# Decode attention with a gated feed-forward: load placement, half-head multiplies, normalisation in pairs and the order of the last loads

## The chip, the cores and the metric

The kernel runs on one core of a Trainium2 chip. The core has a matrix engine (TensorE, "PE" in the profile, its weight loads "PEld"), a vector engine (VectorE, "DVE"), a scalar engine (ScalarE, "ACT"), GpSimd ("POOL") and SyncE ("SP"), which here issues nearly all transfers. Sixteen DMA engines move data between the main memory (HBM) and the on-chip memory (SBUF: 128 partitions); matmul results go to PSUM. The engines run at the same time and wait for each other through semaphores. The metric is the time of one execution on the device in microseconds, as the median of several runs.

## The reference

```python
xn = layernorm(x)                                  # x: 4 x 1 x 640
q = (xn @ wq).reshape(B, 1, 32, 192)               # 32 heads of 192
k, v = k_cache[:, :, 8192 - 2048:, :], v_cache[:, :, 8192 - 2048:, :]
scores = einsum("bhqd,bhkd->bhqk", q, k) * 192 ** -0.5
o = einsum("bhqk,bhkd->bhqd", softmax(scores), v)
A = o.reshape(B, 1, 32 * 192) @ wo
Bf = (silu(xn @ w1) * (xn @ w3)) @ w2              # 640 -> 1536 -> 640
out = x + A + Bf
```

All inputs are bf16. Each of the 4 batch rows has its own K and V for each of 32 heads, and the last 2048 positions count. Per head that is 3 MiB of K and 3 MiB of V for all batch rows, and each is used once.

## The kernel before

The 2048 positions of 4 batch rows lie on 128 partitions: 32 partitions per batch row, 64 positions on each. One head's K is a buffer `kt` of 128 x 64 x 192 (24576 bytes a partition), its V a buffer `vt`; there are two of each, used in turn. The program writes out every engine's order by hand; nothing is scheduled for it.

SP issues the loads (lines 173 to 202). First the projection weights: `wq` into `vt` and `prs` (the product buffer), `w1`, `w3` and `w2` into `wts`; then K0, K1, V0; then for each head h the pair K(h+2), V(h+1), with the first five groups of `wo` put in behind heads 4, 6 and 8; then V31 in two halves and the last three groups of `wo` into `kt0`. `load_k` (L161) waits until three reduces of the head that used the buffer are done, `load_v` (L169) until that head's P x V product is done. The queue is in order: a load that waits holds up all behind it.

The start computes the layer norm on VectorE (L234 to L242, in buffers `xf`, `xc`, `sq`), the transposed input, q for all heads broadcast over the partitions (`qbc`), and the feed-forward, whose result is added up in the PSUM bank `acc` together with x.

Then each head runs through these steps:

- VectorE multiplies a quarter of K by q (`mult`, L266, 128 x 3072), in the two halves of `prs` in turn.
- TensorE adds up the 192 columns to 32 by six matmuls with the identity (`adder`, L435 to L441) into one of two PSUM banks `ps`; VectorE adds up the last 32 (`reduce_quarter`, L273) to 16 scores a partition.
- The maximum: VectorE over the partition (`chain_lmax`, L278), TensorE transposes it (`tr`, L445), VectorE takes the maximum of each batch row and scales it (`chain_gmax`, L282 and L285), TensorE broadcasts it (`bc`, L449), ScalarE copies it (L369).
- ScalarE takes the exponential with its sum (L371), VectorE spreads it into `z` (`chain_z`, L292), TensorE adds up the sums (`tot`, L453) and multiplies `z` by V (`pv`, L458, 32 matmuls).
- ScalarE copies the product (L374); TensorE gathers it by selector matmuls (`osum`, L472, in fp32) into `po`, where the two heads of a pair have columns of their own; VectorE normalises each head (`norm_rec`, L299, `norm_og`, L305) into 32 rows of `og`, and after four heads transposes `og` into `oT` (L309).
- TensorE multiplies `oT` by a group of `wo` into `acc` (`proj`, L399, 12 matmuls a group). Groups 0 to 4 lie among the last two heads (L506 to L525), 5 to 7 behind the last one (L541 to L551).

The steps of one head are put between those of the next: VectorE takes the maximum of head h-1 between the quarters of head h, and the loop of TensorE (L494 to L504) does the same for 28 heads, with the first and the last ones written out. At the very end VectorE copies `acc` to `res` (L352), and SP and ScalarE store half of the columns each (L201, L376). `take` (L138) waits for a semaphore and counts it down again, in an instruction of its own. Semaphores from `s_first` to `s_last` are cleared at the end by GpSimd.

Of the kernel before, what the change touches and what calls it, by code (L numbers as in the profile page):

```python
# [16 lines left out]
def kernel(  # L17
# [58 lines left out]

    kt = [sb(f"kt{i}", [P, NJ, Dh], BF16) for i in range(2)]
    vt = [sb(f"vt{i}", [P, NJ, Dh], BF16) for i in range(2)]
    prs = sb("prs", [P, 2, JQ, Dh], BF16)
# [3 lines left out]
    xf = sb("xf", [B, D], FP32)  # L83
    xc = sb("xc", [B, D], FP32)
    sq = sb("sq", [B, D], FP32)
# [9 lines left out]
    tot_w = sb("tot_w", [P, PB, B], FP32)  # L95
    sel_w = sb("sel_w", [P, 2, PB, B], FP32)
# [12 lines left out]
    rt = sb("rt", [P, 2], FP32)  # L109
# [11 lines left out]
    def sem(name):  # L121
# [4 lines left out]
     s_gp, s_dv, s_ac, s_pp, s_ps, s_red, s_tr, s_gmax, s_bc, s_negm, s_exp, s_pv, s_sum, s_rec, s_og, s_oT,  # L126
     s_tot) = [sem(n) for n in (
        "s_x", "s_wq0", "s_wq1", "s_wq2", "s_w1", "s_w3", "s_w2", "s_k0", "s_k1", "s_v31", "s_wom", "s_wo5",
        "s_wo6", "s_wo7a", "s_wo7b", "s_gp", "s_dv", "s_ac", "s_pp", "s_ps", "s_red", "s_tr", "s_gmax", "s_bc",
        "s_negm", "s_exp", "s_pv", "s_sum", "s_rec", "s_og", "s_oT", "s_tot")]  # L130
    last = sem("s_last")
    s_pr, s_lmax, s_gneg, s_z, s_v0, s_v1, s_osb, s_acc, s_fin, s_out0, s_out1 = [sem(n) for n in (
        "s_pr", "s_lmax", "s_gneg", "s_z", "s_v0", "s_v1", "s_osb", "s_acc", "s_fin", "s_out0", "s_out1")]
# [6 lines left out]
    def flat(t):  # L140
        return t[:].rearrange("p a b -> p (a b)")

    wq_rows = [flat(vt[k // 2])[:, (k % 2) * H * Dh:(k % 2 + 1) * H * Dh] for k in range(4)]
    wq_rows.append(prs[:].rearrange("p a j d -> p (a j d)"))
# [13 lines left out]
    def load_k(h):  # L158
        if h >= 2:
            sp.wait_ge(s_red, 4 * (h - 2) + 3)  # L160
        sp.dma_start(out=flat(kt[h % 2]), in_=k_win[:, h].rearrange("b (p j) d -> p b (j d)", p=PB)).then_inc(s_k[h % 2], 16)  # L161
# [20 lines left out]
    for h in range(H - 2):  # L182
        load_k(h + 2)
        if h + 1 < H - 1:
            load_v(h + 1)
        if h in (4, 6, 8):
            g = h - 4
            n = 2 if g < 4 else 1
            sp.wait_ge(s_pp, 16)
            sp.dma_start(out=wts[g // 2][:, 0:n * RPP * D].rearrange("p (g i) -> p g i", g=n),  # L190
                         in_=A_wo[g * QW:(g + n) * QW, :].rearrange("(g p i) n -> p g (i n)", g=n, i=RPP)).then_inc(s_wom, 16)
    load_v(H - 1, 0, NJ // 2)
    load_v(H - 1, NJ // 2, NJ, s_v31)
    sp.wait_ge(s_red, 4 * (H - 2) + 3)
# [5 lines left out]
    take(sp, s_fin, 1)  # L200
    sp.dma_start(out=out_v[:, 0:N0], in_=res[0:B, :]).then_inc(s_out0, 16)  # L201
    take(sp, s_out0, 16)
# [21 lines left out]
    dv(ve.memset, one[:], 1.0)  # L224
    dv(ve.memset, acc[:, 0:N0], 0.0)
# [4 lines left out]
    dv(ve.tensor_copy, out=tot_w[:], in_=mask_f[:].unsqueeze(1).to_broadcast([P, PB, B]))  # L230
    for par in range(2):
        dv(ve.tensor_copy, out=sel_w[:, par], in_=rows[:, par * B:(par + 1) * B].unsqueeze(1).to_broadcast([P, PB, B]))
    ve.wait_ge(s_x, 16)
    dv(ve.tensor_copy, out=xf[:], in_=x_sb[:])  # L234
    dv(ve.tensor_reduce, out=ssum[:], in_=xf[:], axis=AX.X, op=ALU.add)
    dv(ve.tensor_scalar_mul, out=negmean[:], in0=ssum[:], scalar1=-1.0 / D)
    n_xc = dv(ve.tensor_scalar_add, out=xc[:], in0=xf[:], scalar1=negmean[:, 0:1])
# [4 lines left out]
    n_xn = dv(ve.tensor_scalar_mul, out=xn[:], in0=xc[:], scalar1=rstd[:, 0:1])  # L242
# [19 lines left out]
    def mult(u):  # L262
        h, g = u // GQ, u % GQ
        if g == 0:
            ve.wait_ge(s_k[h % 2], 16 * (h // 2 + 1))
        ve.tensor_tensor(out=prs[:, u % 2], in0=kt[h % 2][:, g * JQ:(g + 1) * JQ, :],  # L266
                         in1=qbc[:, h * Dh:(h + 1) * Dh].unsqueeze(1).to_broadcast([P, JQ, Dh]),
                         op=ALU.mult).then_inc(s_pr, 1)

    def reduce_quarter(u):  # L270
        h, g = u // GQ, u % GQ
        ve.wait_ge(s_ps, u + 1)
        ve.tensor_reduce(out=sc[h % 3][:, g * JQ:(g + 1) * JQ], in_=ps[u % 2][:].rearrange("p (j d) -> p j d", d=DD),  # L273
                         axis=AX.X, op=ALU.add).then_inc(s_red, 1)

    def chain_lmax(h):
        ve.wait_ge(s_red, GQ * (h + 1))
        ve.tensor_reduce(out=lmax[h % 2][:], in_=sc[h % 3][:], axis=AX.X, op=ALU.max).then_inc(s_lmax, 1)  # L278

    def chain_gmax(h):  # L280
        ve.wait_ge(s_tr, h + 1)
        ve.tensor_reduce(out=gmax[h % 2][:], in_=mt[0:1, 0:P].rearrange("o (p b) -> o b p", b=B), axis=AX.X,  # L282
                         op=ALU.max).then_inc(s_gmax, 1)
        ve.wait_ge(s_gmax, h + 1)
        ve.tensor_scalar_mul(out=gneg[h % 2][:], in0=gmax[h % 2][:].unsqueeze(1).to_broadcast([1, PB, B]),  # L285
                             scalar1=-SCALE).then_inc(s_gneg, 1)

    def chain_z(h):
        if h >= 2:
            ve.wait_ge(s_pv, h - 1)  # L290
# [4 lines left out]
    def po_of(h):  # L295
        return po if h < H - 2 else tb

    def norm_rec(c0, c1):
        ve.reciprocal(out=rt[:, c0:c1], in_=po[:, 2 * Dh + c0:2 * Dh + c1]).then_inc(s_rec, c1 - c0)  # L299

    def norm_og(h):
        sl = slice((h % HG) * CT, (h % HG + 1) * CT)
        ve.wait_ge(s_sum, h + 1)
        ve.wait_ge(s_rec, h + 1 if h >= H - 2 else h // 2 * 2 + 2)
        ve.tensor_scalar_mul(out=og[sl].rearrange("p i r -> p (i r)"), in0=po_of(h)[sl, (h % 2) * Dh:(h % 2 + 1) * Dh],  # L305
                             scalar1=rt[sl, h % 2:h % 2 + 1]).then_inc(s_og, 1)
        if h % HG == HG - 1:
            ve.wait_ge(s_og, h + 1)
            ve.transpose(out=oT[:, h // HG].rearrange("p i r -> p (i r)"), in_=flat(og)).then_inc(s_oT, 1)  # L309

    def norm(i):
        ve.wait_ge(s_sum, 2 * i + 2)
        norm_rec(0, 2)
        norm_og(2 * i)
        norm_og(2 * i + 1)

    for h in range(H):
        u, hp = h * GQ, h - 1
        if h < H - 1:
            mult(u)  # L320
        if h:
            reduce_quarter(u - 1)
            chain_lmax(hp)
        if h == H - 1:
            chain_gmax(hp)
            chain_z(hp)
            mult(u)
        mult(u + 1)
        reduce_quarter(u)
        if 0 < h < H - 1:  # L330
            chain_gmax(hp)
        mult(u + 2)
        reduce_quarter(u + 1)
        if h % 2 and 1 < h < H - 1:
            norm(h // 2 - 1)
        if 0 < h < H - 1:
            chain_z(hp)
        mult(u + 3)
        reduce_quarter(u + 2)
    norm(NP - 2)  # L340
    reduce_quarter(H * GQ - 1)
    chain_lmax(H - 1)
    chain_gmax(H - 1)
    ve.wait_ge(s_tot, 1)
    norm_rec(0, 1)
    norm_og(H - 2)
    chain_z(H - 1)
    ve.wait_ge(s_tot, 2)
    norm_rec(1, 2)
    norm_og(H - 1)  # L350
    take(ve, s_acc, 1)
# [6 lines left out]
    ae.activation(out=sq[:], in_=xc[:], func=ACTF.Square, accum_out=ssq[:]).then_inc(s_ac, 1)  # L358
# [8 lines left out]
    for h in range(H):  # L367
        ae.wait_ge(s_bc, h + 1)
# [6 lines left out]
    take(ae, s_fin, 1)  # L375
    ae.dma_start(out=out_v[:, N0:D], in_=res[CT:CT + B, :]).then_inc(s_out1, 16)  # L376
    take(ae, s_out1, 16)


    take(gp, s_fin, 1)  # L380
# [54 lines left out]
    def adder(g):  # L435
        take(pe, s_pr)
        pe.ldweights(idb[:])  # L437
        pr = prs[:, g % 2]
# [8 lines left out]
    def bc(par):  # L447
        take(pe, s_gneg)
        pe.matmul(mt[:, P:P + 1], lhsT=gneg[par][:].rearrange("o p b -> o (p b)"), rhs=one[:], start=True,  # L449
                  stop=True).then_inc(s_bc, 1)  # L450

    def tot(par):
        return pe.matmul(po[:, 2 * Dh + par:2 * Dh + par + 1], lhsT=flat(tot_w), rhs=rsum[par][:], start=True, stop=True)  # L453

    def pv(par, j0=0, j1=NJ):
        for jj in range(j0 // 2, j1 // 2):
# [6 lines left out]
    def tot_pv(par):  # L463
        take(pe, s_z)
        tot(par)
        take(pe, s_v[par], 16)
        pv(par)

    def osum(par, bank):
        take(pe, s_osb)  # L470
        for k in range(2):
            m = pe.matmul(bank[:, par * Dh:(par + 1) * Dh], lhsT=sel_w[:, k].rearrange("p a b -> p (a b)"),  # L472
                          rhs=o_sb[par][:, k * Dh:(k + 1) * Dh].rearrange("p (r i) -> p i r", i=RPP), start=(k == 0), stop=(k == 1))
# [8 lines left out]
    for g in range(5):  # L482
        adder(g)
# [4 lines left out]
    tot_pv(0)  # L488
# [5 lines left out]
    with pe.While(lambda: pe.snap(cnt) < NP - 1):  # L494
        for par in range(2):
            adder(0)
            tr(1 - par)
            osum(par, po)
# [3 lines left out]
            tot_pv(1 - par)  # L502
            adder(3)
        pe.reg_add(cnt, cnt, 1)  # L504

    pe.wait_ge(s_wom, 48)  # L506
    pe.wait_ge(s_oT, 5)
    adder(0)
    tr(1)
    osum(0, po)  # L510
    adder(1)
    bc(1)
    proj(0)
    adder(2)
    tot_pv(1)
    adder(3)
    proj(1)
    tr(0)
    bc(0)
    osum(1, po)  # L520
    proj(2)
    proj(3)
    adder(0)
    adder(1)
    proj(4)  # L525
    adder(2)
    take(pe, s_z)
    take(pe, s_v0, 16)
    pv(0)
    adder(3)  # L530
    osum(0, tb)
    tr(1)
    tot(0).then_inc(s_tot, 1)
    bc(1)
    take(pe, s_z)
    tot(1).then_inc(s_tot, 1)
    take(pe, s_v1, 16)
    pv(1, 0, NJ // 2)
    pe.wait_ge(s_v31, 16)
    pv(1, NJ // 2, NJ)  # L540
    pe.wait_ge(s_oT, 7)  # L541
    pe.wait_ge(s_wo5, 16)
    osum(1, tb)
# [38 lines left out]
```

## Time and profile before

| | us |
|---|---|
| median of 3 runs (lowest, highest) | 532.81 (532.72, 533.38) |
| the profiled execution | 532.96 |
| its span, first to last instruction | 530.8 |
| busy: PE, PEld | 358.6, 99.0 |
| busy: VectorE, ScalarE | 361.7, 44.4 |
| bytes read from HBM | 222.96 MB, 420 GB/s over the span |

The profile is one execution. Its page has busy times, the span in 40 slices, the DMA queues and the costliest groups of instructions; other views list instructions in order of time, waits, and busy times of a chosen window. A group's line names its source line, engine and operation, what it writes and reads, shape and count, then busy us and mean ns of one, then the engine's idle time before it and what ended most of that. The granted clock is the share of full speed that TensorE is given; over the span it was 0.858.

### The profile page before, as it was taken

The numbers are of one execution on the slowest core, as the hardware profiler recorded it, in microseconds if no ns is written. First come the engines' busy times: TensorE is split into PE (matmuls) and PEld (weight loads), VectorE is DVE, ScalarE is ACT, GpSimd is POOL, SyncE is SP. The second block draws the span as 40 slices with busy tenths as digits, with TensorE's granted clock in tenths as the row PEclk, the third lists the DMA queues.
The fourth block names the chain that finished last, engine by engine and source line by source line (L and its number), as shares of the span: only waits on it lengthen the run. The fifth ranks groups of instructions, "written<-read, shape, count | busy, mean of one in ns | idle before, by whom it ended". The sixth has DMA issues, their size and how long they took to land. (4 is left out here: it accounts for less than half of the span.)

```text
span 530.8 us, 5131 instructions
## 1 busy us (share of the span) xinstructions
PE 358.6 (68%) x2306; PEld 99.0 (19%) x1617; DVE 361.7 (68%) x468; ACT 44.4 (8%) x142; POOL 1.1 (0%) x8
## 2 busy tenths in 40 slices
PE   2664767767387473777667666677777667666996
PEld 0010112112022121222111121122221112121323
DVE  3135878768377584768777676767778677767781
ACT  2120100000000000000000000000001000000100
POOL 0000000000000000000000000000000000000000
PEclk9896997878878697888978788888879778889997
DMA  8999999999999999999999999999999999999993
GB/s 356 421 438 425 427 429 428 437 424 423 436 435 421 437 417 436 433 426 435 428 433 430 435 428 430 431 428 433 428 433 426 433 428 431 430 430 433 429 414 132
DMA packets 11522, 223.08 MB, mean 420 GB/s; under 512 B 1260, under 2 KB 1400, under 8 KB 2424
## 3 DMA queue, kind: packets, MB, share of 16 engines
q1 hardware_dynamic: 11496, 222.96, 98.3%
q8 instruction: 4, 0.07, 0.0%
q14 instruction: 6, 0.05, 0.0%
q10 hardware_dynamic: 16, 0.01, 0.0%
HBM read 222.96 MB, written 0.01 MB: 420 GB/s over the span
## 5 line engine op out<-in xcount | busy, mean ns | idle before, releaser
L387 PE MATMUL ps<-prs,idb 128*128 128x512 bf16 x768 | 222.5, 433 | 135.3 <-PEq L138 135.3
L266 DVE TENSOR_TENSOR prs<-kt,qbc 128x3072 bf16<-128x3072 bf16 x128 | 223.7, 1749 | 102.7 <-DMA kt<-in_A_k_cache_dram 102.7
L273 DVE TENSOR_REDUCE sc<-ps 128x16 f32<-128x512 f32 x128 | 87.9, 687 | 18.1 <-PE ps L387 17.0
L437 PEld LDWEIGHTS <-idb 128*128 128x128 bf16 x128 | 13.1, 102 | 197.3 <-issue 195.6
L458 PE MATMUL o_ps<-vt,z 128*8 128x384 bf16 x1024 | 47.3, 327 | 0.0
L472 PE MATMUL po<-o_sb,sel_w 128*128 128x192 f32 x120 | 46.3, 519 | 0.0
L369 ACT COPY negm<-mt 128x1 f32<-128x1 f32 x32 | 5.1, 159 | 347.4 <-PE mt L449 347.4
L472 PEld LDWEIGHTS po<-o_sb,sel_w 128*128 128x128 f32 x120 | 31.0, 286 | 11.0 <-issue 7.0
L458 PEld LDWEIGHTS o_ps<-vt,z 128*8 128x8 bf16 x1024 | 22.0, 86 | 14.2 <-issue 1.3
L374 ACT COPY o_sb<-o_ps 128x384 f32<-128x384 f32 x32 | 15.3, 479 | 101.6 <-PE o_ps L458 101.6
L449 PEld LDWEIGHTS mt<-one,gneg 1*128 1x128 f32 x64 | 9.4, 182 | 58.1 <-issue 58.1
L453 PE MATMUL po<-rsum,tot_w 128*128 128x1 f32 x64 | 10.9, 239 | 12.9 <-PEq L138 12.9
L453 PEld LDWEIGHTS po<-rsum,tot_w 128*128 128x128 f32 x64 | 9.9, 188 | 51.2 <-issue 51.1
L292 DVE TENSOR_TENSOR z<-ex,mask_b 128x256 bf16<-128x256 bf16 x32 | 13.2, 414 | 6.3 <-ACT ex L371 6.0
L220 DVE CAST qbc<-ps 128x512 bf16<-128x512 f32 x2 | 1.4, 692 | 19.1 <-PE ps L387 19.1
L305 DVE TENSOR_SCALAR og<-po,rt 32x192 bf16<-32x192 f32 x30 | 12.4, 413 | 2.1
L445 PEld LDWEIGHTS mt<-idf,lmax 128*1 128x1 f32 x32 | 3.6, 113 | 50.5 <-issue 50.5
L449 PE MATMUL mt<-one,gneg 1*128 1x1 f32 x64 | 12.0, 255 | 1.3 <-PEq L138 1.3
L445 PE MATMUL mt<-idf,lmax 128*1 128x128 f32 x32 | 12.2, 380 | 0.2 <-PEq L138 0.2
L371 ACT ACTIVATE ex<-sc,negm 128x64 bf16<-128x64 f32 x32 | 11.2, 349 | 1.0
L387 PE MATMUL ps<-vt,xnT 128*128 128x512 bf16 x15 | 6.2, 504 | 5.4 <-DMA vt<-in_A_wq_dram 3.8
L282 DVE TENSOR_REDUCE gmax<-mt 1x4 f32<-1x128 f32 x32 | 8.6, 270 | 1.0 <-PE mt L445 1.0
(70 smaller groups left out, 94.8 us busy)
## 6 DMA issues: line engine op xcount, KB each, us to landing
kt<-in_A_k_cache_dram SPq DMA_DIRECT2D x32, 3072.0 KB, 18.0
vt<-in_A_v_cache_dram SPq DMA_DIRECT2D x31, 3072.0 KB, 24.7
vt<-in_A_wq_dram SPq DMA_DIRECT2D x2, 3072.0 KB, 13.4
wt<-in_B_w_dram SPq DMA_DIRECT2D x3, 1920.0 KB, 28.1
wt<-in_A_wo_dram SPq DMA_DIRECT2D x2, 1920.0 KB, 31.2
vt<-in_A_v_cache_dram SPq DMA_DIRECT2D x2, 1536.0 KB, 16.8
kt<-in_A_wo_dram SPq DMA_DIRECT2D x2, 960.0 KB, 20.7
prs<-in_A_wq_dram SPq DMA_DIRECT2D x1, 1536.0 KB, 20.0
```

What stands on the lines that cost most here:

```text
L266: ve.tensor_tensor(out=prs[:, u % 2], in0=kt[h % 2][:, g * JQ:(g + 1) * JQ, :], in1=qbc[:, h * Dh:(h + 1) * Dh].unsqueeze(1).to_broadcast( ...
L273: ve.tensor_reduce(out=sc[h % 3][:, g * JQ:(g + 1) * JQ], in_=ps[u % 2][:].rearrange("p (j d) -> p j d", d=DD), axis=AX.X, op=ALU.add).the ...
L292: ve.tensor_tensor(out=z[h % 2][:], in0=ex[h % 2][:].unsqueeze(2).to_broadcast([P, NJ, B]), in1=mask_b[:].unsqueeze(1).to_broadcast([P, NJ ...
L305: ve.tensor_scalar_mul(out=og[sl].rearrange("p i r -> p (i r)"), in0=po_of(h)[sl, (h % 2) * Dh:(h % 2 + 1) * Dh], scalar1=rt[sl, h % 2:h % ...
L374: ae.copy(out=o_sb[h % 2][:], in_=o_ps[h % 2][:, 0:2 * Dh]).then_inc(s_osb, 1)
L387: return pe.add_instruction(mybir.InstMatmult(name=nc.get_next_instruction_name(), engine=pe.engine, ins=[pe.lower_ap(rhs), pe.lower_ap(lh ...
L437: pe.ldweights(idb[:])
L445: pe.transpose(out=mt[0:1, 0:P], in_=lmax[par][:], identity=idf[:]).then_inc(s_tr, 1)
L449: pe.matmul(mt[:, P:P + 1], lhsT=gneg[par][:].rearrange("o p b -> o (p b)"), rhs=one[:], start=True, stop=True).then_inc(s_bc, 1)
L453: return pe.matmul(po[:, 2 * Dh + par:2 * Dh + par + 1], lhsT=flat(tot_w), rhs=rsum[par][:], start=True, stop=True)
L458: m = pe.matmul(o_ps[par][c * CT:c * CT + 2 * B, 0:2 * Dh].rearrange("p (a d) -> p a d", a=2), lhsT=z[par][:, 2 * jj:2 * jj + 2, :], rhs=v ...
L472: m = pe.matmul(bank[:, par * Dh:(par + 1) * Dh], lhsT=sel_w[:, k].rearrange("p a b -> p (a b)"), rhs=o_sb[par][:, k * Dh:(k + 1) * Dh].re ...
```

## The change

- A pad in front of the buffers puts `kt0`, and with it all loaded buffers, at a multiple of 512 bytes in each partition. `xf`, `xc` and `sq` now lie in `qbc`, which is written later.
- `prs` is twice as large. A multiply covers half a head (128 x 6144), and `s_m` counts multiplies. `load_k` waits for the two multiplies of the head that used the buffer. TensorE's `adder` no longer waits for the multiply itself but for the reduce behind it in VectorE's order (`s_pr` for quarters 0 and 2).
- The scaling of the maximum goes from VectorE to ScalarE, behind a wait for `s_gmax`.
- The sums and the selector products of two heads are added up in the same PSUM columns, each head in its own 32 rows (`tot_w` and `sel_w` have zeros elsewhere), so that one reciprocal and one 64-row multiplication normalise both.
- K31 is issued behind K30, ahead of V29 and V30. TensorE's written-out end has another order: the projection of group 0 ahead of V29's product, groups 1 to 4 around the last head's maximum.
- The last waits (`s_acc`, `s_fin`) stand in the instructions that need them; the counting down comes after the store.

```diff
+    sb("pad", [P, -((nc.sbuf_base + 31) // 32 * 32) % 512 // 2], BF16)
     kt = [sb(f"kt{i}", [P, NJ, Dh], BF16) for i in range(2)]
     vt = [sb(f"vt{i}", [P, NJ, Dh], BF16) for i in range(2)]
-    prs = sb("prs", [P, 2, JQ, Dh], BF16)
+    prs = sb("prs", [P, 2, 2, JQ, Dh], BF16)
...
-    xf = sb("xf", [B, D], FP32)
-    xc = sb("xc", [B, D], FP32)
-    sq = sb("sq", [B, D], FP32)
+    xf, xc, sq = [qbc[0:B, 2 * i * D:2 * (i + 1) * D].bitcast(FP32) for i in range(3)]
...
     def load_k(h):
         if h >= 2:
-            sp.wait_ge(s_red, 4 * (h - 2) + 3)
+            sp.wait_ge(s_m, 2 * (h - 2) + 2)
...
     for h in range(H - 2):
         load_k(h + 2)
-        if h + 1 < H - 1:
+        if h < H - 4:
             load_v(h + 1)
...
+    load_v(H - 3)
+    load_v(H - 2)
     load_v(H - 1, 0, NJ // 2)
     load_v(H - 1, NJ // 2, NJ, s_v31)
-    sp.wait_ge(s_red, 4 * (H - 2) + 3)
+    sp.wait_ge(s_m, 2 * (H - 2) + 2)
...
-    take(sp, s_fin, 1)
+    sp.wait_ge(s_fin, 1)
     sp.dma_start(out=out_v[:, 0:N0], in_=res[0:B, :]).then_inc(s_out0, 16)
+    take(sp, s_fin)
...
+    dv(ve.memset, tot_w[:], 0.0)
+    dv(ve.memset, sel_w[:], 0.0)
...
     for par in range(2):
-        dv(ve.tensor_copy, out=sel_w[:, par], in_=rows[:, par * B:(par + 1) * B].unsqueeze(1).to_broadcast([P, PB, B]))
+        dv(ve.tensor_copy, out=quads(tot_w[:, par], par), in_=mask_f[:].unsqueeze(1).unsqueeze(1).to_broadcast([P, 2, PQ, B]))
+        for k in range(2):
+            dv(ve.tensor_copy, out=quads(sel_w[:, par, k], par),
+               in_=rows[:, k * B:(k + 1) * B].unsqueeze(1).unsqueeze(1).to_broadcast([P, 2, PQ, B]))
...
+    def mult(h, a):
+        if a == 0:
             ve.wait_ge(s_k[h % 2], 16 * (h // 2 + 1))
+        ve.tensor_tensor(out=prs[:, a].rearrange("p q j d -> p (q j) d"), in0=kt[h % 2][:, 2 * a * JQ:2 * (a + 1) * JQ, :],
+                         in1=qbc[:, h * Dh:(h + 1) * Dh].unsqueeze(1).to_broadcast([P, 2 * JQ, Dh]),
+                         op=ALU.mult).then_inc(s_m, 1)
...
+    def norm_rec(i):
+        ve.reciprocal(out=rt[:], in_=tb[:, 0:1]).then_inc(s_rec, 1)
+
+    def norm_og(i):
+        sl = slice(i % 2 * 2 * CT, (i % 2 + 1) * 2 * CT)
+        ve.wait_ge(s_rec, i + 1)
+        ve.tensor_scalar_mul(out=og[sl].rearrange("p i r -> p (i r)"), in0=po[sl, 0:Dh], scalar1=rt[sl, 0:1]).then_inc(s_og, 1)
...
     for h in range(H):
+        mult(h, 0)
         if h:
+            reduce_quarter(h - 1, 2)
+            reduce_quarter(h - 1, 3)
+            chain_lmax(h - 1)
+        mult(h, 1)
+        if h:
+            chain_gmax(h - 1)
+        reduce_quarter(h, 0)
+        reduce_quarter(h, 1)
+        if h % 2 and h > 1:
+            norm_rec(h // 2 - 1)
+            norm_og(h // 2 - 1)
+        if h:
+            chain_z(h - 1)
...
-    take(ve, s_acc, 1)
+    ve.wait_ge(s_acc, 1)
...
     for h in range(H):
+        ae.wait_ge(s_gmax, h + 1)
+        ae.mul(out=gneg[h % 2][:], in_=gmax[h % 2][:].unsqueeze(1).to_broadcast([1, PB, B]), mul=-SCALE).then_inc(s_gneg, 1)
         ae.wait_ge(s_bc, h + 1)
...
     def adder(g):
-        take(pe, s_pr)
+        if g % 2 == 0:
+            take(pe, s_pr)
+        add_up(g)
+
+    def add_up(g):
         pe.ldweights(idb[:])
-        pr = prs[:, g % 2]
+        pr = prs[:, g // 2, g % 2]
...
+    adder(0)
+    tr(1)
+    osum(0)
+    adder(1)
+    bc(1)
+    adder(2)
+    tot(1)
+    adder(3)
     pe.wait_ge(s_wom, 48)
     pe.wait_ge(s_oT, 5)
+    proj(0)
+    pv(1)
     adder(0)
+    tr(0)
+    osum(1)
+    adder(1)
+    bc(0)
+    adder(2)
+    tot(0)
+    adder(3)
+    pv(0)
+    proj(1)
     tr(1)
+    proj(2)
     bc(1)
+    osum(0)
     proj(3)
     proj(4)
     tot(1).then_inc(s_tot, 1)
     pv(1, 0, NJ // 2)
     pe.wait_ge(s_v31, 16)
     pv(1, NJ // 2, NJ)
+    osum(1)
     pe.wait_ge(s_oT, 7)
     pe.wait_ge(s_wo5, 16)
-    osum(1, tb)
     proj(5)
```

## The prediction

> **What bounds the kernel now.** I read the transfer rows first, because the slices show them full from end to end.
>
> ```profile
> DMA  8999999999999999999999999999999999999993
> GB/s 356 421 438 425 427 429 428 437 424 423 436 435 421 437 417 436 433 426 435 428 433 430 435 428 430 431 428 433 428 433 426 433 428 431 430 430 433 429 414 132
> ...
> q1 hardware_dynamic: 11496, 222.96, 98.3%
> ...
> q14 instruction: 6, 0.05, 0.0%
> ```
>
> Only the first and the last slice fall away; SP's queue (q1) keeps 16 engines 98.3% busy. By the landings of consecutive loads, 3 MiB take 7.304 us again and again (8 packets of 24576 bytes per engine, 912 ns each, plus one of 4 bytes, 9 ns). A head is a K and a V, 14.6 us. Next, who could starve that queue:
>
> ```profile
> SPq L161 <- DVE sc L273: 417.4, 30, 21.6
> ...
> SPq L169 <- PE o_ps L458: 11.4, 1, 11.4
> ...
> L266 DVE TENSOR_TENSOR prs<-kt,qbc 128x3072 bf16<-128x3072 bf16 x128 | 223.7, 1749 | 102.7 <-DMA kt<-in_A_k_cache_dram 102.7
> ...
> L305 DVE TENSOR_SCALAR og<-po,rt 32x192 bf16<-32x192 f32 x30 | 12.4, 413 | 2.1
> ```
>
> SP waits for VectorE to release a K buffer, yet the engines never pause, since a load still runs when the next is issued; VectorE itself waits 102.7 us for K. So VectorE, TensorE and ScalarE time inside the 30 middle heads is worth nothing. What is left is the bytes' rate, and the end, read in short windows (columns: length, busy us and counts of PE, PEld, DVE, ACT, POOL, granted clock, DMA share, GB/s) and in the timeline:
>
> ```profile
> 520.00:522.00 2.00, 1.33 (x14) 0.78 (x7) 0.00 (x0) 0.48 (x1) 0.00 (x0) 0.54 0.76 306
> 522.00:523.00 1.00, 1.00 (x5) 0.49 (x6) 0.00 (x0) 0.00 (x0) 0.00 (x0) 0.50 0.24 95
> 523.00:524.00 1.00, 1.00 (x10) 0.46 (x9) 0.81 (x2) 0.00 (x0) 0.00 (x0) 0.50 0.06 26
> 524.00:525.00 1.00, 1.00 (x10) 0.46 (x8) 0.00 (x0) 0.00 (x0) 0.00 (x0) 0.50 0.06 23
> 525.00:526.00 1.00, 1.00 (x10) 0.53 (x8) 0.00 (x0) 0.00 (x0) 0.00 (x0) 0.50 0.00 0
> ```
>
> ```profile
> 518.99 1.65 PE L458 MATMUL o_ps<-vt,z 128*8 128x384 bf16 x32
> ...
> 520.68 0.48 ACT L374 COPY o_sb<-o_ps 128x384 f32<-128x384 f32 x1 [2.65 <-PE o_ps L458]
> ...
> 521.30 1.68 PE L472 MATMUL tb<-o_sb,sel_w 128*128 128x192 f32 x4 [0.67 <-PEq L138]
> 522.91 4.59 PE L399 MATMUL acc<-kt,oT 128*4 128x320 bf16 x36
> ...
> 527.65 0.48 DVE L352 CAST res<-acc 36x320 bf16<-36x320 f32 x1 [3.79 <-DVEq L138]
> 528.25 0.35 SPq L201 DMA_DIRECT2D out_dram<-res  x1
> ```
>
> From 523 to 525 a share of 0.06 is one engine of 16: one runs late by 2.1 us. The last weights (issued at 502.92, 22.6 us to landing) are there at 525.5, but TensorE ends at 527.5: from 520.16 it has half the clock, and 36 matmuls take 4.59 us. At the full clock 12 of these took 0.98 and 24 took 1.79, so 36 would take 2.6.
>
> **The change, part by part.** The sum is made against the profiled execution, 532.96 us (span 530.8, 2.2 around it), 0.15 above the median of 532.81.
>
> *Work taken off VectorE: 0.* Two multiplies of 6144 for four of 3072 save about 0.08 a head (two in a row took 3.42, not 2 x 1.75); the scaled maximum goes to ScalarE (32 x 215 ns less); one 64-row normalisation replaces two of 32 (half of 12.4 us). All lies under VectorE's 102.7 us of waiting for K. A head needs about 2 x 3.42 + 4 x 0.69 + 0.22 + 0.27 + 0.41 + 0.4 = 10.9 us of 14.6. The price of coarser pieces is that TensorE's first sum starts 1.7 us later after a landing, inside the spare 3.7 us; beyond that it would be paid each head. ScalarE's new wait for the maximum stands behind the copy of the previous head's output and before the negated maximum and the exponential, which TensorE's order needs in that sequence anyway.
>
> *Buffers released by the multiply:* K is free about 8.4 us after its landing (3.42 + 1.6 of reduces and maximum + 3.42) rather than about 11. Nothing, since no engine pauses now.
>
> *Prelude: 0.* Two memsets and four more small copies (about 0.2-0.3 each, as L220's rows) put roughly 1.3 us before the layer norm. TensorE there waited 1.26 us for the first weights, which covers it but for 0.1; the next weights come 7 us later and swallow that.
>
> *Multiples of 512.* The program's addresses put kt0 at 16512 = 32 x 512 + 128 and every loaded buffer at the same remainder; a pad of 384 bytes makes it 0. No run here has a load at remainder 0. Bound: packets of 24576 and 12288 bytes took 912 and 460 ns, so a packet costs 2 x 460 - 912 = 8 ns beyond its bytes (27.2 GB/s per engine). Each engine moves 10240 / 16 = 640 packets: at most 5.1 us to gain. The other end is 0: the 4-byte packets cost 9 ns with nothing to place. A loss I exclude, as all buffers move together. The nearest rows are 1280-byte packets to two places, 53 ns (x, remainder 128) and 55 ns (end of the last weights, 384): 2 ns. I take 2 x 640 = **-1.3 us**.
>
> [...]
>
> *Fewer instructions: -0.9 us.* VectorE's list goes from 560 to 376. Instruction packets of 8192 bytes came at 192, 311 and 428 us, about every 130 VectorE instructions; beside each, one data packet took about 1570 ns for 912, and the fetch 325: 1.0 us on the late engine. At 10.3 instead of 15.6 instructions a head there are two, not three, before the end. Ends: 0 (ScalarE's 32 more fetched there too) and -1.0.
>
> *K31 before V29, and TensorE's new end: -1.4 us.* The two swap places: K31 lands near 496.5, V29 at 503.9 (K31's place, issued 486.98, 16.9 to landing). Queues: K31's issue needs both multiplies of head 29, 474.6 + 8.4 = 483.0, first packet 1.0 later (as at the start, issue 0.96, first packet 2.0); the quick engines finish K30 at 484.9, 0.9 to spare, the late one 2.2 more. V31 stands behind V29's product on SP, and the last weights behind V31: V29 503.9 + 1.5, first packet 506.4, V30 done at 506.8 on the quick engines. Tight, but the late engine sets the end. Then TensorE by start to start in the timeline (product 1.41, sum 1.30, selector sum 1.34, transpose 0.18, broadcast 0.30, total 0.28, projection 0.81): from 503.94, product 29, four sums, transpose, selector sum and broadcast, with the wait for z, bring the last sum to an end at 512.9; product 30 514.3; projection 1, transpose, projection 2, broadcast 516.4; selector sum 517.8; projections 3 and 4 519.4; total, product 31 521.1; ScalarE's copy 521.7; selector sum 523.3; 36 matmuls 525.8. The last weights at 525.1 and 525.5 then hold it to about 526.1, for 527.5. V31's wait is gone from this chain; the weights' landing is late next.
>
> This needs the full clock. In these windows of 3.41 us the clock falls after one with little TensorE work:
>
> ```profile
> 472.37:475.78 3.41, 0.00 (x0) 0.00 (x0) 1.14 (x1) 0.00 (x0) 0.00 (x0) 1.00 0.99 425
> ...
> 513.34:516.75 3.41, 3.08 (x17) 1.29 (x8) 2.14 (x7) 0.48 (x1) 0.00 (x0) 1.00 1.00 417
> 516.75:520.16 3.41, 1.80 (x36) 1.27 (x36) 1.21 (x5) 0.60 (x3) 0.00 (x0) 1.00 1.02 422
> 520.16:523.57 3.41, 2.74 (x18) 1.48 (x12) 0.51 (x2) 0.48 (x1) 0.00 (x0) 0.50 0.47 185
> ```
>
> Product, projections and selector sums now fill 513 to 520 almost wholly, so it should hold.
>
> *Fused waits: -0.15 us.* The last cast starts 0.15 after TensorE, a fused wait 0.04 (516.30 to 516.34); the store 0.12 after the cast, about half of it to save. SP's added decrement lies under the store's 2 us.
>
> Sum: 532.96 - 1.3 - 0.9 - 1.4 - 0.15 = 529.2, against the median **529.1 us**.
>
> **Rivals.**
> 1. *Placement is the whole 8 ns:* 529.1 + 1.3 - 5.1 = 525.3. For it: the 8 ns is the same for all large sizes; against: the 4-byte packets.
> 2. *Only the end changes:* no gain from placement, instruction fetches as late as now: 532.81 - 1.4 - 0.15 = 531.3; and if the clock still drops at 520.16, the end is pushed from 521.1 by 1.65 - 1.41, copy, 1.68 and 4.59 to about 528.5, 1.0 above now: 533.7, no change. For it: the clock fell there before.
> 3. *Slower: projections 3 and 4 and a selector sum, now between the last maximum and product 31, run at half clock.* It decides if the window 513.34:516.75 holds less than about 1.5 us of TensorE work, through a late V30 for instance. Then 24 matmuls cost 3.06 for 1.79 and the selector sums 0.16 each more, and rival 2's cold end follows: 533.7 + 1.6 = 535.3. Against it: 3.08 us in that window now, and more work moved in.
>
> **How the numbers follow.** Forecast 529.1 (own range 527 to 531) 0.52; rival 1 and what lies near it 0.16; rival 2 0.24, a third of it under 531.7, a sixth at the cold end's 533.7; rival 3 0.08. This kernel's measurement tells 0.2%, 1.07 us, from no change. Faster 0.52 + 0.16 + 0.08 = 0.76; same 0.16; slower 0.08. The range 525.8 to 533.2 leaves out half of rival 1, rival 3 and the cold end, 0.20 together.
>
> **What would show it.** A 24576-byte load at 910 ns a packet is my step, 912 says placement is nothing, 904 rival 1. The gap between the late engine and the others at the end should be near 1.1 us; TensorE's last 36 matmuls at clock 1.00; DMA share 0.99 or more between 484 and 510. A pause of the queue there, or a granted clock of 0.50 after 513, makes the prediction wrong.

## The result, and the profile after

The changed kernel took **528.39 us** (median of 4 executions, 528.23 to 528.73) beside 533.1 us for the kernel before (4 executions, 532.72 to 534.08): ratio 0.991, 95% interval 0.9893 to 0.9927. Measured a second time (E9) it took 528.5 us (527.99 to 528.72, 6 executions), ratio 0.9919, interval 0.9894 to 0.9944. Forecast was 529.1.

The profiled execution took 528.51 us with a span of 525.7 (before: 532.96 and 530.8). The span fell by 5.2 us, the time by 4.45; the 0.74 between them is taken up below.

First the transfers, from the page of the changed kernel (slices, then the queues with packets, MB and share of 16 engines):

```profile
DMA  8999999999999999999999999999999999999995
GB/s 358 422 440 423 438 428 434 434 426 426 439 438 428 434 422 442 428 439 425 439 425 439 428 438 428 434 432 430 438 426 441 426 435 430 438 428 434 432 419 211
...
q1 hardware_dynamic: 11496, 222.96, 98.8%
...
q14 instruction: 5, 0.04, 0.0%
```

The same packets and bytes still fill 16 engines from end to end, 98.8% of a shorter span. The queue became hardly fuller: it became faster. The mean time from one load's landing to the next (by the middle engine, the eighth of the 16 to land, over 40 loads in a row) fell from 7.305 to 7.272 us. And q14 shows 5 instruction packets instead of 6.

Next SyncE's waits in the changed kernel (us in total, times, longest), and two groups of VectorE:

```profile
SPq L160 <- DVE prs L276: 289.5, 30, 18.7
SPq L168 <- PE o_ps L452: 144.6, 29, 15.7
```

```profile
L276 DVE TENSOR_TENSOR prs<-kt,qbc 128x6144 bf16<-128x6144 bf16 x64 | 214.5, 3353 | 110.4 <-DMA kt<-in_A_k_cache_dram 110.4
...
L305 DVE TENSOR_SCALAR og<-po,rt 64x192 bf16<-64x192 f32 x16 | 6.7, 416 | 4.0 <-PE po L460 3.5
```

SyncE now waits for the multiply itself, and the product with V holds it 29 times where it held it once. Both belong to an engine ahead of a full queue. VectorE's wait for K grew from 102.7 to 110.4 us: what it saved it now spends waiting.

The end, in the timeline of the changed kernel (start, length, what; in brackets the idle time before it):

```profile
516.14 1.47 PE L452 MATMUL o_ps<-vt,z 128*8 128x384 bf16 x32
...
517.67 0.48 ACT L360 COPY o_sb<-o_ps 128x384 f32<-128x384 f32 x1 [4.36 <-PE o_ps L452]
518.29 1.58 PE L460 MATMUL po<-o_sb,sel_w 128*128 128x192 f32 x4 [0.68 <-PEq L137]
519.80 2.61 PE L386 MATMUL acc<-kt,oT 128*4 128x320 bf16 x36
...
522.52 0.48 DVE L336 CAST res<-acc 36x320 bf16<-36x320 f32 x1 [1.77 <-PE acc L386]
523.03 0.35 SPq L202 DMA_DIRECT2D out_dram<-res  x1
```

and in short windows (length, then busy us and count of PE, PEld, DVE, ACT, POOL; granted clock, DMA share, GB/s):

```profile
484.00:510.00 26.00, 21.03 (x176) 5.87 (x123) 21.79 (x23) 2.77 (x10) 0.00 (x0) 1.00 1.00 428
...
513.34:516.75 3.41, 3.41 (x45) 1.86 (x47) 0.59 (x2) 0.00 (x0) 0.00 (x0) 1.00 1.01 422
516.75:520.16 3.41, 2.73 (x34) 1.27 (x24) 0.25 (x1) 0.48 (x1) 0.00 (x0) 1.00 0.70 286
520.16:523.57 3.41, 2.25 (x34) 1.24 (x29) 1.04 (x3) 0.00 (x0) 0.00 (x0) 1.00 0.02 6
```

The last 36 matmuls take 2.61 us at clock 1.00 for 4.59 at 0.50. The last weights are complete at 521.37, and the matmuls run through without a wait for them: TensorE's own chain is last, 1.04 us after the weights. The middle engine brought these weights at 519.16 (before 522.15), the late one at 521.37 (before 525.50); the late engine is 2.21 behind the middle one, no longer 3.35.

### The profile page after: what moved, and what is told of

The parts are those of the page before. It is cut to its first block, busy times and chain, and to the rows that moved or that the text cites. A ratio compares the mean times of both kernels' runs of the same rounds, so it can differ in the third digit from the quotient of the medians.

```text
span 525.7 us, 4915 instructions
## 1 busy us (share of the span) xinstructions
PE 358.6 (68%) x2307; PEld 98.3 (19%) x1617; DVE 342.0 (65%) x360; ACT 54.2 (10%) x174; POOL 1.1 (0%) x8
## 3 DMA queue, kind: packets, MB, share of 16 engines
q1 hardware_dynamic: 11496, 222.96, 98.8%
## 5 line engine op out<-in xcount | busy, mean ns | idle before, releaser
L374 PE MATMUL ps<-prs,idb 128*128 128x512 bf16 x768 | 225.8, 439 | 136.7 <-PEq L137 129.8
L276 DVE TENSOR_TENSOR prs<-kt,qbc 128x6144 bf16<-128x6144 bf16 x64 | 214.5, 3353 | 110.4 <-DMA kt<-in_A_k_cache_dram 110.4
L282 DVE TENSOR_REDUCE sc<-ps 128x16 f32<-128x512 f32 x128 | 84.2, 681 | 28.1 <-PE ps L374 27.9
L460 PE MATMUL po<-o_sb,sel_w 128*128 128x192 f32 x128 | 49.4, 520 | 0.7 <-PEq L137 0.7
L353 ACT ACTIVATE gneg<-gmax 1x128 f32<-1x128 f32 x32 | 9.8, 308 | 303.5 <-DVE gmax L291 303.5
L460 PEld LDWEIGHTS po<-o_sb,sel_w 128*128 128x128 f32 x128 | 32.9, 284 | 12.6 <-issue 8.3
L445 PEld LDWEIGHTS tb<-rsum,tot_w 128*128 128x128 f32 x64 | 9.5, 188 | 44.3 <-issue 44.3
L445 PE MATMUL tb<-rsum,tot_w 128*128 128x1 f32 x64 | 11.3, 246 | 4.2 <-PEq L137 4.1
L305 DVE TENSOR_SCALAR og<-po,rt 64x192 bf16<-64x192 f32 x16 | 6.7, 416 | 4.0 <-PE po L460 3.5
```

The source lines that it names most:

```text
L276: ve.tensor_tensor(out=prs[:, a].rearrange("p q j d -> p (q j) d"), in0=kt[h % 2][:, 2 * a * JQ:2 * (a + 1) * JQ, :], in1=qbc[:, h * Dh:(h ...
L374: return pe.add_instruction(mybir.InstMatmult(name=nc.get_next_instruction_name(), engine=pe.engine, ins=[pe.lower_ap(rhs), pe.lower_ap(lh ...
L445: return pe.matmul(tb[:, 0:1], lhsT=flat(tot_w[:, par]), rhs=rsum[par][:], start=(par == 0), stop=(par == 1))
L460: m = pe.matmul(po[:, 0:Dh], lhsT=flat(sel_w[:, par, k]), rhs=o_sb[par][:, k * Dh:(k + 1) * Dh].rearrange("p (r i) -> p i r", i=RPP), star ...
```

## The experiments

Times are medians of n executions; "before" ran beside them on the same chip (535.04 us for E1 to E4, 533.14 for E5, E6 and E8, 532.45 for E9 to E11). "us per load" is the step from one full load's landing to the next; "last weights" and "TensorE ends" are times in the profiled execution. There is no E7.

| | kernel | us (range, n) | ratio to before, 95% interval | us per load | last weights | TensorE ends |
|---|---|---|---|---|---|---|
| | before, first profile | 532.81 (532.72–533.38, 3) | | 7.305 | 525.50 | 527.50 |
| | changed, first profile | 528.39 (528.23–528.73, 4) | 0.991, 0.9893–0.9927 | 7.272 | 521.37 | 522.41 |
| E1 | before + pad | 530.99 (528.51–533.68, 10) | 0.9925, 0.9903–0.9947 | 7.272 | 522.37 | 524.96 |
| E2 | changed, remainder 128 | 531.27 (531.24–531.64, 4) | 0.9942, 0.9924–0.9959 | 7.304 | 525.14 | 525.86 |
| E3 | changed, remainder 256 | 528.35 (527.93–528.92, 4) | 0.989, 0.987–0.9909 | 7.272 | 521.58 | 523.01 |
| E4 | changed, remainder 64 | 531.66 (530.86–531.89, 4) | 0.9944, 0.9924–0.9964 | 7.305 | 524.99 | 525.69 |
| E5 | changed, V29 before K31 | 532.56 (532.04–533.7, 10) | 0.9989, 0.9969–1.0009 | 7.272 | 521.38 | 526.30 |
| E6 | changed + 180 VectorE instructions | 529.59 (529.35–530.28, 9) | 0.9933, 0.9908–0.9958 | 7.272 | 522.57 | 523.28 |
| E8 | changed, two projections later | 527.37 (527.29–528.16, 6) | 0.9898, 0.9868–0.9928 | 7.272 | 521.50 | 522.22 |
| E9 | changed, again | 528.5 (527.99–528.72, 6) | 0.9919, 0.9894–0.9944 | 7.272 | 521.59 | 522.62 |
| E10 | E8, again | 527.35 (527.26–528.12, 6) | 0.9902, 0.9876–0.9927 | 7.272 | 521.58 | 522.29 |
| E11 | before, again | 535.03 (1) | | 7.305 | 525.36 | 529.56 |

**E1: the kernel before, with the pad alone.**

```diff
+    sb("pad", [P, -((nc.sbuf_base + 31) // 32 * 32) % 512 // 2], BF16)
     kt = [sb(f"kt{i}", [P, NJ, Dh], BF16) for i in range(2)]
```

> The kernel before with the 384-byte pad alone. Theory (placement is a price per packet, about 4 ns as the loads of the changed kernel suggest: 7.272 us for 3 MiB against 7.305): 7.27 us a load, 640 packets x 4.1 ns = 2.6 us, time about 530.3 where the kernel before has 533.0. Rival (the loads are quicker because fewer instructions are fetched or because K is released earlier): 7.305 us a load and 533. The prediction's 2 ns would give 531.7.

The load falls from 7.305 to 7.272 us in a kernel that has nothing else of the change, and the queue's last landing from 525.50 to 522.37: the pad does this alone. In time the medians differ by 4.0 us (by the interval, 2.8 to 5.2), more than the 2.6 us of the packets. Both kernels scatter by 4 to 5 us (E11 shows from what), so how much of that is the pad's own can't be read here.

**E2, E3, E4: the changed kernel with its buffers at other remainders of 512.**

```diff
-    sb("pad", [P, -((nc.sbuf_base + 31) // 32 * 32) % 512 // 2], BF16)
+    sb("pad", [P, ((128 - (nc.sbuf_base + 31) // 32 * 32) % 512 or 512) // 2], BF16)
```

(128 in E2; 256 in E3 and 64 in E4.)

> The changed kernel with its buffers back at remainder 128. Theory: 7.305 us a load, time 528.4 + 2.6 = 531.0, and the rest of the gain (1.8 to 2) stays. Rival (placement nothing): 528.4.

> The changed kernel at remainder 256. If a 256-byte boundary is what counts: 7.27 us a load and 528.4, as at 0. If it is 512: 7.305 and 531.0.

> The changed kernel at remainder 64. If a packet pays for the bytes between the boundary and its start, 64 bytes are half of what 128 cost: about 2 ns a packet, 529.7. If any start off the boundary costs the same (one more transaction): 531.0.

Remainders 0 and 256 give 7.272 us a load, 64 and 128 give 7.305 and 7.304, and the times fall into the same two groups: E3's 528.35 lies on the changed kernel's 528.39, E2 and E4 are 2.9 and 3.3 us slower than E3 (their spans 2.8 and 2.7 us longer in the profiles). So a boundary of 256 bytes counts, not 512. A load is 8 packets an engine, so being off it costs 33 / 8 = 4.1 ns a packet, and equally for 64 and 128 bytes. Not all of E2's 2.9 us are packets: V29 is complete at 502.90 for E3's 500.04, and on the middle engine at 499.85 for 497.46. That is 2.4 us; the other 0.5 is the late engine, 3.05 us behind the middle one for 2.58.

A price by the bytes between the boundary and the start would have cost remainder 64 half as much as remainder 128 (E4's first case). The runs don't show that: 7.305 us beside 7.304. What the flat price consists of, nothing here measures; the "one more transaction" of E4's expectation was my guess.

In E2's timeline the last projection no longer runs through:

```profile
521.35 1.58 PE L460 MATMUL po<-o_sb,sel_w 128*128 128x192 f32 x4 [0.68 <-PEq L137]
522.86 1.79 PE L386 MATMUL acc<-kt,oT 128*4 128x320 bf16 x24
524.88 0.98 PE L386 MATMUL acc<-kt,oT 128*4 128x320 bf16 x12 [0.22 <-DMA kt<-in_A_wo_dram]
```

The selector sum starts 3.06 us later than in the changed kernel (518.29), as V29 landed 3.06 us later, and the last 12 matmuls then wait 0.22 us for the weights: with slower packets it is the transfer that sets the end. The clock is at full in both (1.00).

**E5: the changed kernel, with V29 in front of K31 as before.**

```diff
-        if h < H - 4:
+        if h < H - 2:
             load_v(h + 1)
...
-    load_v(H - 3)
-    load_v(H - 2)
     load_v(H - 1, 0, NJ // 2)
```

> The changed kernel with V29 loaded before K31 again (TensorE's order as changed). Theory: K31 lands 7.3 us later, near 499.8, and head 31's first multiply waits for it where it started at 495.6, so the last maximum, z and the end come about 4 us later: 532. Rival (the weights' landing sets the end anyway): 528.4 to 529.

The queue ends at the same instant (521.38 for 521.37), and TensorE 3.89 us later: the end is a matter of order alone. E5's timeline, first VectorE, then TensorE, then the window of the slow sum:

```profile
499.87 3.36 DVE L274 TENSOR_TENSOR prs<-kt,qbc 128x6144 bf16<-128x6144 bf16 x1 [3.30 <-DMA kt<-in_A_k_cache_dram]
```

```profile
499.06 1.54 PE L450 MATMUL o_ps<-vt,z 128*8 128x384 bf16 x28
503.98 2.72 PE L372 MATMUL ps<-prs,idb 128*128 128x512 bf16 x6 [3.38 <-PEq L137]
506.49 0.36 PE L434 MATMUL mt<-idf,lmax 128*1 128x128 f32 x1
```

```profile
503.25:506.67 3.42, 2.69 (x7) 0.41 (x3) 3.39 (x4) 0.00 (x0) 0.00 (x0) 0.50 0.96 408
```

and the same place in the changed kernel:

```profile
495.60 3.35 DVE L276 TENSOR_TENSOR prs<-kt,qbc 128x6144 bf16<-128x6144 bf16 x1
```

```profile
499.98 1.47 PE L452 MATMUL o_ps<-vt,z 128*8 128x384 bf16 x32 [1.57 <-PEq L137]
501.38 1.47 PE L374 MATMUL ps<-prs,idb 128*128 128x512 bf16 x6
```

Either way the last full load is complete at 499.84 or 499.85. If it is K31, a multiply of 3.36 us stands between it and TensorE, which runs dry for 3.38 us and then does its first sum at half clock (0.50 in the window): 2.60 us later at the start of that sum and 1.25 more for it, 3.85 together. If it is V29, only a product of 1.4 us stands there, and K31's first half is long multiplied. Without the swap all the rest of the change is worth nothing that this measurement tells: ratio 0.9989, interval 0.9969 to 1.0009. (E5 keeps TensorE's new order, which was written for the swap; the swap with the old order was not run.)

**E6: the changed kernel with 180 more instructions for VectorE.** Six one-element memsets a head, into a tile that nothing reads:

```diff
+        if h < H - 2:
+            for i in range(6):
+                ve.memset(junk[:, 6 * h + i:6 * h + i + 1], 0.0)
```

> The changed kernel with 6 tiny memsets of VectorE (into a tile that nothing reads) in each of heads 0 to 29, 180 instructions more, so that VectorE's list is as long as before. Theory: one more instruction fetch on the late engine, its lag behind the middle engine at the end 3.2 us instead of 2.2, the time 0.7 to 1.0 longer: 529.2. The 11 us of extra VectorE work cost nothing. Rival (TensorE's chain alone sets the end, and the late engine does not reach it): 528.4. Other rival (VectorE's time is not free): more than 531.

VectorE's instruction fetches of 8192 bytes come at 169, 290 and 402 us; the changed kernel had two, at 246 and 425, and the kernel before three, at 192, 312 and 428 (from 100 us on; the rows name no engine, but the kernel before runs 130 VectorE instructions from one to the next, the changed one 128). Every fetch but the first leaves the late engine 0.9 to 1.0 us further behind the middle one, and most of that stays (in the changed kernel 2.48 us after the second fetch, 2.33 at V29, 72 us later). After each fetch the lag is 1.5, 2.4 and 3.2 us in E6; 1.5 and 2.4 in the changed kernel; 1.7, 2.7 and 3.7 in the kernel before.

The first fetch added at most 0.2 to the lag in these three (0.5 in E4), but it cost its engine as much. In the kernel before, the last three of the 16 engines land 0.75, 1.41 and 1.53 us behind the middle one in the load ahead of that fetch, and 1.42, 1.51 and 1.73 in the load it falls into. The landings don't name their engines; the reading that moves only one of them is that the engine at 0.75 lost 1.0 us and so became the last. The later fetches then add to the lag itself.

V29 is complete at 500.71 for 499.84, and TensorE starts its product and ends 0.87 us later too (523.28 for 522.41): it is this landing that the time follows. V31's loads wait for V29's product:

```profile
503.00:506.00 3.00, 3.00 (x14) 0.92 (x6) 2.85 (x3) 0.31 (x1) 0.00 (x0) 1.00 0.96 386
506.00:509.00 3.00, 2.98 (x16) 0.70 (x6) 2.20 (x5) 0.60 (x3) 0.00 (x0) 1.00 0.94 343
```

These are E6's windows; the changed kernel's dip less:

```profile
503.00:506.00 3.00, 3.00 (x13) 0.92 (x6) 1.80 (x4) 0.35 (x2) 0.00 (x0) 1.00 0.97 407
506.00:509.00 3.00, 2.98 (x18) 0.38 (x11) 1.85 (x5) 0.56 (x3) 0.00 (x0) 1.00 0.97 412
```

343 GB/s for 412 over 3 us is half a microsecond of all engines. On the middle engine V30 still lands at 504.92 for 504.78, but the first half of V31 at 509.40 for 508.47: the quick engines ran out of work before V31 was issued. So this fetch is paid on every engine, not on one: the last weights' middle landing is 520.11 for 519.16. The time is 1.1 to 1.2 us up by the medians (528.39 and 528.5 were not measured beside E6), the profiled span 0.9.

**E8, E9, E10: two projections moved behind the last product**, so that they run while ScalarE copies it.

```diff
-    proj(3)
-    proj(4)
...
+    proj(3)
...
+    proj(4)
```

(Projection 3 now stands in front of the last selector sum, projection 4 behind it.)

> The changed kernel with projections 3 and 4 moved behind the last product: 3 beside ScalarE's copy, 4 behind the last selector sum. In the changed kernel's trace TensorE is idle 0.68 us beside that copy, and the weights have landed 1.0 us before it ends. Theory (TensorE's chain sets the end now): 0.4 to 0.7 us less, 527.8. Rival (the weights' landing sets it): 528.4.

> The changed kernel a second time, on the same chip as the kernel with the late tail. My reading: it ends by TensorE's own chain, about 1.0 us after the last weights land, so TensorE ends near 522.4 and its last 36 matmuls wait for no transfer; 528.2 to 528.7 us again, scatter under 1 us. Rival, that the first measurement was a lucky chip: over 530.

> The late tail a second time, beside the changed kernel on one chip. If moving projections 3 and 4 behind the last product takes work off the chain that ends the kernel, it is 0.5 to 1.3 us faster than the changed kernel beside it and its last matmuls wait for the weights' landing. Rival, that the 527.4 was only the scatter between chips: equal to the changed kernel within 0.3 us.

E10's timeline:

```profile
518.95 1.80 PE L386 MATMUL acc<-kt,oT 128*4 128x320 bf16 x24
521.32 0.98 PE L386 MATMUL acc<-kt,oT 128*4 128x320 bf16 x12 [0.57 <-DMA kt<-in_A_wo_dram]
```

Side by side on one chip this kernel takes 527.35 us for the changed kernel's 528.5: the fastest here. But the reason is only in part the one I had. TensorE gets ahead of the weights and then waits 0.57 us for them; its end moves from 522.62 to 522.29, 0.33 us, and the span by 0.33. The profiled executions differ by 1.33 (528.72 and 527.39): the other 1.0 lies outside the span. That is no accident of one execution: time less span is 1.8 to 1.9 us in all 12 executions of E8 and E10, and 2.4 to 2.8 in all 10 of the changed kernel. Why is open.

**E11: the kernel before, once more**, for its scatter.

> The kernel before, one more profile, to see where its scatter of 4 us between executions comes from. If it is TensorE's clock at the end, the last projection's 36 matmuls take either 4.6 us at half clock (as in the first profile) or 2.6 us at full clock, and the time follows by about 2 us, with the last weights' landing unchanged near 525.5. If it is the queue, the landing moves with the time.

TensorE around the first sum of head 30, in E11 and then in the first profile, and the end of E11:

```profile
491.01 2.37 PE L387 MATMUL ps<-prs,idb 128*128 128x512 bf16 x6 [3.57 <-PEq L138]
```

```profile
491.16 1.46 PE L387 MATMUL ps<-prs,idb 128*128 128x512 bf16 x6 [3.29 <-PEq L138]
```

```profile
518.99 0.43 DVE L292 TENSOR_TENSOR z<-ex,mask_b 128x256 bf16<-128x256 bf16 x1 [0.67 <-ACT ex L371]
...
519.56 0.56 PE L453 MATMUL po<-rsum,tot_w 128*128 128x1 f32 x2 [1.34 <-PEq L138]
...
520.05 2.73 PE L458 MATMUL o_ps<-vt,z 128*8 128x384 bf16 x32
...
525.07 4.49 PE L399 MATMUL acc<-kt,oT 128*4 128x320 bf16 x36
```

The expectation was half right. The landing stayed (525.36 for 525.50) and the time is 2.07 us longer, so it is not the queue. But the 36 matmuls ran at half clock both times. What differs is when else the clock was down. In E11 it was at 0.50 from 491.40 to 494.81, and the sum there took 2.37 us for 1.46; from there on TensorE is 0.86 us later (517.87 for 517.01 at the last maximum's broadcast). Then the clock fell at 518.71, within TensorE's idle 1.34 us in front of the last product, which took 2.73 us; in the first profile it fell at 520.16, when most of that product was done (1.65 us). The last 36 matmuls so start 2.16 us later (525.07 for 522.91). The end of the kernel before hangs on when the clock happens to fall; with the pad alone (E1) the last 36 matmuls had full clock in the profile (2.61 us). The changed kernel kept the full clock from before 500 to TensorE's end in each of its two profiles, and its executions lie within 0.75 us.

## Why the prediction was right, and where it was not

**VectorE's work, earlier release, prelude: 0.** Held, as far as shown; none of the three was run alone. VectorE's saving turned into 7.7 us more waiting for K; E6's 180 extra instructions cost only what their fetches do to the queue. The first query product waited 0.23 us for the layer norm's result (forecast 0.1).

**Multiples of 512: forecast -1.3, measured -2.6 to -2.9.** This is the term that was mis-sized. My bounds of 0 and 5.1 held; I took 2 ns a packet from the nearest small packets, and it is 4.1: 640 x 4.1 = 2.6 us on the queue. E2 and E3, on one chip, differ by 2.9 in time. By the loads, a packet is (7272 - 9) / 8 = 908 ns against the three values that I had named, 912, 910 and 904: between my step and rival 1. The packets' own rows must not be read for this sign: 8242 of the 8320 large ones show 912 ns in the changed kernel, which by my list would have said "nothing"; in the kernel before they mostly show 912 to 921, with a mean of 917.7 for 913.8. The small 1280-byte packets told little, since both places that I compared, 128 and 384, are off the 256-byte boundary. Remainder 256 would have done as well.

**Fewer instructions: forecast -0.9, right.** Two fetches for three, as said. The late engine's lag behind the middle one fell by 1.1 us at the last weights (3.35 to 2.21) and by 1.4 at V29 (3.70 to 2.33); behind the next engine it is 0.76, where I had named 1.1 as the sign. One fetch given back (E6) costs 0.9 in the span and 1.1 to 1.2 in time.

**K31 before V29 and the new end: forecast -1.4.** The mechanism held: the clock stayed at full, the DMA share between 484 and 510 was 1.00, and V31's wait left the chain. From the start of V29's product to TensorE's end I had 526.1 - 503.9 = 22.2 us and it took 522.41 - 499.98 = 22.4. (V29 stands in K31's former place, 503.84 before, 499.84 now.) One step was wrong: "the weights' landing is late next". The weights landed 21.5 us after V29, as forecast, but the chain was longer than my sum of its parts and ended 1.04 us behind them; the landing is late next only with slower packets (E2) or a shorter tail (E8). The net term hid how much stands on the swap: E5 shows that without it the rest of the new order would lose what packets and fetches gain.

**Fused waits: forecast -0.15.** The cast starts 0.11 us after TensorE for 0.15, the store's issue 0.03 after the cast for 0.12: 0.13 us of the span.

**Not foreseen: 0.74 us outside the span**, 2.86 for 2.12 us. With it the sum closes. Beside the forecast, V29 lands 1.3 us earlier by the packets (middle engine 497.51, before 500.14: 2.6 for 1.3) and 0.5 by the late engine's lag (1.4 for 0.9); the chain behind it takes 0.3 more, and 0.74 more lies outside: -1.3 - 0.5 + 0.3 + 0.7 = -0.8, and 528.51 lies 0.7 under the summed 529.2. So 529.1 came this close in part by luck: the gains were 1.8 us larger than forecast, and 1.0 us that I had not foreseen stood against them.

The 0.74 compares one execution with one. Time less span is 2.1 to 3.4 us over the executions of the kernel before that ran beside E1 to E11, and 2.4 to 2.8 over the 10 of the changed kernel, so how much of it the change brings is open.

What lies outside goes with something that the trace shows: in the profiles of the changed kernel, E9, E1, E2, E4, E5 and E6 an instruction fetch is recorded after the span's end, and 2.5 to 3.0 us lie outside; in those of the kernel before, E11, E3, E8 and E10 none is, and it is 1.85 to 2.1. E3 has the changed kernel's instructions, so the code's length doesn't decide it alone. That the fetch is the cause was not tried.

**Rivals.** The whole 8 ns (525.3) falls: 4.1. Only the end changes (531.3 or 533.7) falls: E1 shows the packets' gain and E6 the fetch's. Half clock before the last product (535.3) did not come in the changed kernel, though E5's clock fell while TensorE stood dry for 3.38 us, and the kernel before ran its last product at half clock in E11.

## What to carry to other kernels

Where a queue of large transfers is full from end to end, look at what each packet costs beyond its bytes: here starting on a 256-byte boundary was worth 2.6 to 2.9 us of 531, by one line that shifts an allocation. Load last the operand that needs the least work before the next engine can start: here the same bytes in the other order gave back all the rest (E5). And weigh a change to an engine that isn't the bound by what it does to the queue too: its instructions are fetched through the same engines as the data (here each fetch of 8192 bytes cost one engine about 1.0 us).

## What the runs showed of the hardware

- A destination 64 or 128 bytes off a 256-byte boundary costs the same 4.1 ns a packet of 24576 bytes (7.305 and 7.304 us a load for 7.272 at 0 and 256).
- An instruction fetch of VectorE's, 8192 bytes, leaves one DMA engine 0.9 to 1.0 us behind, and in a full queue little of that is made up (2.48 to 2.33 us over 72 us). The first one hardly shows in the lag of the last engine (0.1 to 0.2 us in three profiles), by the reading given with E6 because the engine it fell to was not yet the last: 0.75 us behind the middle one before it, 1.73 after.
- Two profiles of one kernel with nearly equal landings of the last weights (525.36 and 525.50) differ by 2.07 us by the clock alone: in the slower one it was also at half from 491.40 to 494.81, and at the end it fell at 518.71 for 520.16, around the same two idle stretches of TensorE (0.59 and 1.34 us). In the profiles of the kernel before and of the changed one all 112 stretches of one clock, without the last of each, take 3.41 us or a whole multiple of it (the half one from 520.16 takes 6.83); so do the half ones from 518.71 in E11 (10.24) and from 488.99 in E10 (3.41). The falls at 518.71 and 520.16 lie 1.45 us apart, no multiple of 3.41, so they don't keep one place counted from the kernel's start; these two executions show what that alone can be worth. In the kernel before, 3.41 us at full clock with at most 1.32 us of TensorE work were followed by half clock and those with 1.45 or more by full clock, but for the 1.80 us in front of 520.16; in the changed kernel the two sides are 1.27 and 1.42.
